# Row sums of a softmax gradient: from TensorE and PSUM to VectorE and SBUF, with a new instruction order for the whole program

## The chip, the core and the metric

The kernel runs on one core of one Trainium2 chip. Five engines of that core work side by side, each through its own list of instructions, in the order of that list: TensorE (PE, matmuls, which write PSUM), VectorE (DVE), ScalarE (ACT), GpSimd (POOL) and SyncE (SP, which here only starts transfers). The metric is the device time of one execution in microseconds (us), from the first to the last instruction and the little that lies around them. Lower is better.

## What is computed

The program is one transformer layer, forward, and the gradients of its inputs and weights. Sequence 2048, width 512, 32 heads of 16; each position attends to 8 positions, itself and those 2, 4, ... 14 before it.

```python
qkv = layernorm(x) @ wqkv                       # q, k, v per head
logits[h,s,w] = (q[h,s] . k[h,s-2w]) * scale    # w = 0..7, masked before the start
attn = softmax(logits, over w)
h  = x + (sum_w attn[h,s,w] * v[h,s-2w]) @ wo
h2 = h + gelu(layernorm(h) @ w1 + b1) @ w2 + b2
# outputs: h2 and the gradients of x, wqkv, wo, w1, b1, w2, b2 for a given grad_out
```

The change lies in the backward softmax. With `da[h,s,w] = (grad of the attention output at s) . v[s-2w]`, the gradient of the logits is

```
pp = attn * da
glf = pp - attn * sum_w(pp)         which equals  attn * (da - sum_w pp)
```

## The kernel before

The 2048 rows are four chunks of 512. Per chunk the program has three stages. The forward attention stage makes the layer norm, q, k, v (`p1_qkv`), the logits and softmax (`p1_attn`), the weighted sum of v (`p1_o`) and h (`p1_h`). The MLP stage runs the MLP forward and backward (`p2_h`, `p2_out`, `p2_dg`, `p2_bwd`); its end is `ln_bwd` (L604 to L617), which leaves the gradient of h in the tile `ghr`. The last stage is the attention backward: `p3_go` (L946) multiplies `ghr`, turned by a DMA transpose, by wo and leaves `got`; `p3_dots` makes the softmax gradient; `p3_bands` makes the gradients of q, v and k; `p3_gl1` (L1045) brings them back to x, and `ln_bwd` finishes the tile `gx`, which is stored. The weight gradients (`wg_group`, L1071) are long accumulating matmuls that need no VectorE; they are placed between everything else.

No 8-wide dot product is a matmul here. VectorE multiplies two wide tiles (128 x 4096, tiles `prf`, `prb`, `prbo`, `prbq`, `prbv`, `prbk`, L517 and L557), and TensorE adds groups of partitions up by a matmul with a constant 0/1 matrix (`S`, L525 and L566), 8 or 16 matmuls of 32 output rows for each such product. A wide product occupies VectorE and is followed by a short matmul group that waits for it.

In `p3_dots`, for one chunk, four products `prb` (L517) and their sums (L525) leave `da` in two PSUM banks, `L`. Then:

- L966, VectorE: `pp` = `L` * `attn`, 1024 elements on 128 partitions, fp32 from PSUM, bf16 to SBUF.
- L972, TensorE: minus the sum of `pp` over w, as eight accumulating 128-column matmuls with `nident`, the negative identity. ScalarE copies the sum to the SBUF tile `sr` (L283, tag `rowsum`).
- L985, TensorE: two 512-column matmuls with `ident` add `sr`, repeated over w, onto `L`.
- L988, VectorE: `glf` = `L` * `attn`, again from PSUM.
- L541, ScalarE: `halos` copies a few columns of `glf` between partitions.

`glf` is transposed in blocks into `cfq` and `cfk` (L535), the factors of the products `prbq` and `prbk`.

What sets the order is no scheduler at run time. The whole program is first listed as small operations (`op`), and two tables of numbers written out at the end of the file decide: `ORDER` gives the order in which the operations are issued, for all engines at once, and `HOMES` the SBUF address or PSUM bank of every tile. Each engine then runs its own operations in that order. A wait arises where an operation needs a result of another engine, or where its tile lies on the place of an older tile that is still being read.

Of the kernel before, what the change touches and what calls it, by code (L numbers as in the profile page):

```python
# [10 lines left out]
P = 128  # L11
# [3 lines left out]
ALU = mybir.AluOpType  # L15
# [3 lines left out]
W = 8  # L19
# [129 lines left out]
def kernel(  # L149
# [105 lines left out]
    MM = 0.2157  # L255
# [5 lines left out]
    def tt_us(n, f32=False):  # L261
        return 0.07 + (1.04e-3 if f32 else 0.52e-3) * n
# [689 lines left out]
    def p3_dots(c):  # L952
# [8 lines left out]
        L = ps_("La", 2)  # L961
# [21 lines left out]
        def sub():  # L983
            for wh in range(2):
                T.matmul(L()[:, wh * 512:(wh + 1) * 512], lhsT=(nident if RSB else ident)[:], rhs=sr().unsqueeze(1).to_broadcast([P, 4, P]), start=False, stop=True,  # L985
                         skip_group_check=True)
        op("PE", 2 * MM, sub, r=[sr, NID if RSB else IDENT], w=[L], tag="subsum")
        op("DVE", tt_us(1024, True), lambda: V.tensor_tensor(out=glf()[:, c, :, 0:P], in0=L3(), in1=ac(), op=ALU.mult),  # L988
           r=[L, (attn, c)], w=[(glf, c)], tag="glf")
# [290 lines left out]
RSB = False  # L1280
# [169 lines left out]
```

## Time and profile before

| what | value |
|---|---|
| runs of the kernel | 544.49, 546.46, 546.56 us; median 546.46 |
| the profiled execution: its own time | 545.53 us |
| the profiled execution: its span | 543.8 us (1.7 us lie around it) |
| mean granted TensorE clock | 0.996 |
| busy: PE, DVE, ACT, POOL | 97%, 86%, 62%, 3% |
| bytes moved by DMA | 136.63 MB, mean 251 GB/s |

All rows that are quoted below come from that one execution. "PE" is matmul time, "PEld" the loading of the stationary matrix, which overlaps it; "SPq" is a transfer being issued. A group row gives the line, the engine, the operation, what it writes and reads, how often (x), its busy time and the mean length of one in ns, then the engine's idle time just in front and what ended it. In a timeline row the first number is the start, the second the length, both in us.

### The profile page before, as it was taken

How to read it: one execution, taken by the hardware profiler on the slowest of the kernel's cores; microseconds unless marked ns; L12 is line 12 of the kernel's file. 1: busy time of each engine (PE TensorE's matmuls, PEld its weight loads, DVE VectorE, ACT ScalarE, POOL GpSimd, SP SyncE). 2: the span in 40 equal slices, each digit the busy share in tenths (PEclk: the TensorE clock that was granted, in tenths of full speed). 3: DMA queues.
4: the chain of work that ended last, by engine and by line, in shares of the span. 5: the costliest groups of instructions: out<-in, count | busy, mean ns of one | idle time of the engine just before them, and what ended most of it. 6: DMA issues, size and time to landing. Idle time of an engine off the chain costs nothing.

```text
span 543.8 us, 8104 instructions
## 1 busy us (share of the span) xinstructions
PE 526.0 (97%) x3017; PEld 235.3 (43%) x3063; DVE 467.7 (86%) x599; ACT 339.0 (62%) x591; POOL 17.4 (3%) x23
## 2 busy tenths in 40 slices
PE   8699999999999999999999999999999999999995
PEld 3344434444444444444444444445544444433442
DVE  5969999999999999998670339899989999999973
ACT  6938878999999967896522423224254455444664
POOL 0310000200000100000000000000000000000003
PEclk9989999999999999999999999999999999999999
DMA  7898899998998999999999999999999899999987
GB/s 216 204 285 250 249 271 296 246 272 253 226 256 252 304 238 221 219 271 204 230 170 204 191 203 212 208 293 257 230 331 303 298 309 233 318 309 287 289 223 220
DMA packets 230872, 136.63 MB, mean 251 GB/s; under 512 B 188400, under 2 KB 218800, under 8 KB 226736
## 3 DMA queue, kind: packets, MB, share of 16 engines
q1 hardware_dynamic: 230448, 135.06, 97.2%
q0 software_dynamic: 384, 1.05, 0.7%
q8 instruction: 24, 0.39, 0.3%
q14 instruction: 16, 0.13, 0.1%
HBM read 54.73 MB, written 37.84 MB: 170 GB/s over the span
## 4 chain that ended last, share of the span: by engine, by line
PE 86%; DVE 4%; DMA 4%; ACT 2%; issue 2%; SPq 1%; POOL 0%; POOLq 0%; DVEq 0%; ACTq 0%
PE ps L1071 27%; PE ps L908 9%; PE ps L922 9%; PE ps L880 9%; PE ps L826 8%; PE ps L1045 8%; PE ps L566 6%; PE ps L674 4%; PE ps L946 3%; DVE prf L517 2%; PE ps L525 2%; DMA w<-in_B_w_dram 2%; PE ps L790 1%; DMA ln1T<-ln 1%; PE ps L699 1%
## 5 line engine op out<-in xcount | busy, mean ns | idle before, releaser
L908 PE MATMUL ps<-goT,w2T 128*128 128x512 bf16 x224 | 52.5, 379 | 0.1
L922 PE MATMUL ps<-w1T,xb 128*128 128x512 bf16 x217 | 51.3, 379 | 0.4
L880 PE MATMUL ps<-w,gl 128*128 128x512 bf16 x218 | 50.8, 379 | 0.7 <-DMA w<-in_B_w_dram 0.3
L826 PE MATMUL ps<-ln2T,w 128*128 128x512 bf16 x224 | 50.3, 379 | 0.1
L1045 PE MATMUL ps<-wqkvT,gqkvT 128*128 128x512 bf16 x187 | 43.7, 380 | 0.6 <-ACT gvs L571 0.2
L283 ACT CAST wgs<-ps 128x512 bf16<-128x512 f32 (+1 forms) x30 | 15.8, 561 | 45.0 <-PE ps L1071 45.0
L828 ACT ACTIVATE xb<-ps,b1c 128x512 bf16<-128x512 f32 x56 | 35.1, 689 | 10.1 <-PE ps L826 9.9
L910 DVE SCALAR_TENSOR_TENSOR xb<-xb,ps 128x512 bf16<-128x512 bf16 x56 | 36.7, 682 | 5.4 <-PE ps L908 4.9
L1071 PE MATMUL ps<-gw1in,ln 128*128 128x512 bf16 (+1 forms) x186 | 38.8, 352 | 0.3
L1071 PE MATMUL ps<-gor,gw2in 128*128 128x512 bf16 x162 | 38.6, 379 | 0.4 <-issue 0.2
L557 DVE TENSOR_TENSOR prbq<-Rq,cfq 128x4096 bf16<-128x4096 bf16 x16 | 36.0, 2287 | 1.4 <-PE ps L566 1.1
L557 DVE TENSOR_TENSOR prbv<-Rv,cfv 128x4096 bf16<-128x4096 bf16 x16 | 35.9, 2286 | 0.4 <-DMA Rv<-go_d 0.3
L557 DVE TENSOR_TENSOR prbo<-Ro,cfo 128x4096 bf16<-128x4096 bf16 x16 | 36.0, 2285 | 0.1
L517 DVE TENSOR_TENSOR prf<-qt,kt 128x4096 bf16<-128x4096 bf16 x16 | 36.0, 2280 | 0.0
L517 DVE TENSOR_TENSOR prb<-got,vw 128x4096 bf16<-128x4096 bf16 x16 | 35.8, 2285 | 0.2
L557 DVE TENSOR_TENSOR prbk<-Rk,cfk 128x4096 bf16<-128x4096 bf16 x16 | 35.8, 2284 | 0.0
L1071 PEld LDWEIGHTS <-ln 128*128 128x128 bf16 x256 | 24.5, 98 | 23.9 <-issue 1.7
L880 PEld LDWEIGHTS <-gl 128*128 128x128 bf16 x224 | 21.7, 98 | 27.4 <-issue 1.5
L908 PEld LDWEIGHTS <-w2T 128*128 128x128 bf16 x224 | 21.9, 98 | 26.6 <-issue 0.4
L922 PEld LDWEIGHTS <-xb 128*128 128x128 bf16 x224 | 21.9, 98 | 26.5
L826 PEld LDWEIGHTS <-w 128*128 128x128 bf16 x224 | 21.5, 98 | 27.3 <-issue 2.4
L604 ACT ACTIVATE gyr<-ps,rstd 128x512 bf16<-128x512 f32 x28 | 19.0, 680 | 18.6 <-PE ps L1045 12.4
(164 smaller groups left out, 924.5 us busy)
## 6 DMA issues: line engine op xcount, KB each, us to landing
Ro<-v_d SPq DMA_DIRECT2D x4, 1280.0 KB, 7.3
Rq<-k_d SPq DMA_DIRECT2D x4, 1280.0 KB, 7.2
Rv<-go_d SPq DMA_DIRECT2D x4, 1280.0 KB, 6.3
Rk<-q_d SPq DMA_DIRECT2D x4, 1280.0 KB, 7.7
g_d<-gl SPq DMA_DIRECT2D x9, 512.0 KB, 4.0
gh_d<-xb SPq DMA_DIRECT2D x9, 512.0 KB, 4.2
Ro<-v_d SPq DMA_DIRECT2D x4, 1024.0 KB, 7.2
Rq<-k_d SPq DMA_DIRECT2D x4, 1024.0 KB, 8.5
```

The costliest lines, as they stand in the source:

```text
L517: op("DVE", tt_us(4096), lambda g=g, pr=pr: V.tensor_tensor(out=pr(), in0=ql()[:, g, :].unsqueeze(1).to_broadcast([P, W, 512]), in1=_sub(k ...
L557: V.tensor_tensor(out=pr().rearrange("p j a (d h) -> p (j a) d h", h=H), in0=_sub(R()[:, o0, 0:1], [[1024, 4], [st, 2], [1, 512]]), in1=_s ...
L566: T.matmul(ps()[32 * j:32 * j + 32, :], lhsT=S4[:], rhs=pr()[:, j, hf, :], start=(hf == 0), stop=(hf == 1), skip_group_check=True)
L674: T.matmul(ps()[:, gg * 512:(gg + 1) * 512], lhsT=_sub(wq_()[:, dc, 0:1], [[4, P]], g), rhs=cols_r(st_[c]["ln1T"], dc) if c in PM else col ...
L826: T.matmul(ps(), lhsT=w1()[:, dc, f * P:(f + 1) * P], rhs=cols(ln2T[c], dc, c in FM2), start=(dc == 0), stop=(dc == DC - 1))
L828: op("ACT", act_us(512, 1), lambda f=f, ps=ps, xb=xb, f0=f0: A.activation(out=xb()[:, f - f0, :], in_=ps(), func=ACT.Identity, bias=b1c[:, ...
L880: T.matmul(ps(), lhsT=d["g"][f // 4]()[:, f % 4, j * P:(j + 1) * P], rhs=w2()[:, f, :], start=(f == 0), stop=(f == FT - 1))
L908: T.matmul(ps(), lhsT=w2T()[:, dc, f * P:(f + 1) * P], rhs=cols(goT, dc, True), start=(dc == 0), stop=(dc == DC - 1))
L910: op("DVE", 0.61, lambda f=f, ps=ps, z=z, f0=f0: V.scalar_tensor_tensor(out=z()[:, f - f0, :], in0=z()[:, f - f0, :], scalar=1.0, in1=ps() ...
L922: T.matmul(ps(), lhsT=d["d"][f // 4]()[:, f % 4, j * P:(j + 1) * P], rhs=w1T()[:, f, :], start=(f == 0), stop=(f == FT - 1))
L1045: T.matmul(ps(), lhsT=gT()[:, j, b * P:(b + 1) * P], rhs=wqkvT()[:, k0 + b, :], start=(i == 0 and b == 0), stop=(i == 2 and b == 3))
L1071: T.matmul(ps()[:, 0:N], lhsT=l, rhs=r, start=(n == 0), stop=(n == k - 1))
```

## The change

The row sum and the subtraction move to VectorE and SBUF. `RSB = True` selects a branch that was there already: VectorE adds `pp` up over w with one `tensor_reduce` into `sr`. The two matmuls that added the sums onto `L`, and the product from PSUM, are replaced by two VectorE operations on bf16 tiles in SBUF: `glf` = `attn` * `sr`, then `glf` = `pp` - `glf`. The PSUM bank of the sums and ScalarE's copy are gone. Both tables are new from the first number to the last, so every engine's list changes, in all stages. In the changed file the lines behind L982 have numbers lower by three.

```diff
-        def sub():
-            for wh in range(2):
-                T.matmul(L()[:, wh * 512:(wh + 1) * 512], lhsT=(nident if RSB else ident)[:], rhs=sr().unsqueeze(1).to_broadcast([P, 4, P]), start=False, stop=True,
-                         skip_group_check=True)
-        op("PE", 2 * MM, sub, r=[sr, NID if RSB else IDENT], w=[L], tag="subsum")
-        op("DVE", tt_us(1024, True), lambda: V.tensor_tensor(out=glf()[:, c, :, 0:P], in0=L3(), in1=ac(), op=ALU.mult),
-           r=[L, (attn, c)], w=[(glf, c)], tag="glf")
+        gl = lambda: glf()[:, c, :, 0:P]
+        op("DVE", tt_us(1024), lambda: V.tensor_tensor(out=gl(), in0=ac(), in1=sr().unsqueeze(1).to_broadcast([P, W, P]), op=ALU.mult),
+           r=[sr, (attn, c)], w=[(glf, c)], tag="glfs", lock=1)
+        op("DVE", tt_us(1024), lambda: V.tensor_tensor(out=gl(), in0=pp(), in1=gl(), op=ALU.subtract), r=[pp], w=[(glf, c)], tag="glf", lock=1)
         halos(glf, c, "g")
...
-RSB = False
+RSB = True
...
 ORDER = (
-    7, 63, 64, 0, 10, 8, 65, 66, 4, 6, 42, 5, 26, 25, 3, 21, 24, 27, 22, 9, 30, 33, 28, 31,
...
 HOMES = (
-    608, 1115, 1883, 1024, 672, 2261, 2485, 1185, 701, 2261, 2117, 320, 1731, 288, 1121, 1603, 1796, 1989, 224, 160, 1925, 192, 128, 1024,
+    1365, 2673, 1925, 1024, 672, 2261, 2485, 1185, 701, 2261, 2117, 320, 1729, 288, 1121, 1603, 1796, 1989, 224, 160, 1601, 224, 128, 288,
```

Two places of VectorE's list show what the tables do around the change. The first is where the last stage begins. This is VectorE's list before; `u` and `ghr` belong to the MLP stage's `ln_bwd`, and `prb` are the first products of the attention backward (two chunks):

```order
L616 TENSOR_TENSOR u_1224_53_2915<-u_1224_53_2915,gor_39_1993 128x1024
L616 TENSOR_TENSOR u_1207_52_2879<-u_1207_52_2879,gor_39_1993 128x1024
L617 TENSOR_TENSOR ghr_1254_50_3002<-u_1128_46_2679,gyr_1020_46_2424 128x1024
L616 TENSOR_TENSOR u_1183_50_2823<-u_1183_50_2823,gor_38_1988 128x1024
L617 TENSOR_TENSOR ghr_1254_50_3002<-u_1183_50_2823,gyr_1061_49_2509 128x1024
L617 TENSOR_TENSOR ghr_1264_44_3021<-u_1224_53_2915,gyr_1150_48_2726 128x1024
L617 TENSOR_TENSOR ghr_1264_44_3021<-u_1207_52_2879,gyr_1151_48_2728 128x1024
L517 TENSOR_TENSOR prb_40_3051<-got_51_2783,vw_49_2473 128x4096
L517 TENSOR_TENSOR prb_41_3053<-got_51_2783,vw_49_2473 128x4096
```

And this is the same place of VectorE's list now:

```order
L617 TENSOR_TENSOR ghr_1240_51_2947<-u_1177_52_2804,gyr_1057_41_2500 128x1024
L517 TENSOR_TENSOR prb_50_2949<-got_53_2819,vw_43_2402 128x4096
L517 TENSOR_TENSOR prb_51_2951<-got_53_2819,vw_43_2402 128x4096
L617 TENSOR_TENSOR ghr_1240_51_2947<-u_1195_54_2843,gyr_1039_50_2472 128x1024
L1240 CAST gbb_46_3030<-gb_48_2788 128x18
L517 TENSOR_TENSOR prb_46_3032<-got_53_2819,vw_43_2402 128x4096
L517 TENSOR_TENSOR prb_47_3034<-got_53_2819,vw_43_2402 128x4096
L960 COPY vw_47_2784<-vw_48_2576 128x4x16
L616 TENSOR_TENSOR u_1237_51_2943<-u_1237_51_2943,gor_39_2164 128x1024
L616 TENSOR_TENSOR u_1230_51_2932<-u_1230_51_2932,gor_39_2164 128x1024
L617 TENSOR_TENSOR ghr_1287_43_3090<-u_1230_51_2932,gyr_1131_49_2685 128x1024
```

The first products have moved ahead of the last additions of the MLP stage, which now stand between and behind them; before, all eight `ghr` additions were through first. In TensorE's list 1,694 matmuls now stand ahead of the first sums of a `prb`, where 1,726 stood; the 32 that moved behind have 512 columns. At the other end, behind the last sums of a `prbk`, 96 matmuls of 512 columns now stand, where 84 stood. In all, TensorE's list has 3,023 matmuls instead of 3,063.

The second place is the softmax gradient of the first chunk on VectorE, before:

```order
L966 TENSOR_TENSOR pp_41_3126<-ps,attn_21_439 128x1024
L517 TENSOR_TENSOR prb_42_3134<-got_43_3059,vw_47_2488 128x4096
L517 TENSOR_TENSOR prb_42_3151<-got_43_3059,vw_47_2488 128x4096
L517 TENSOR_TENSOR prb_40_3171<-got_43_3059,vw_47_2488 128x4096
L988 TENSOR_TENSOR glf_39_3187<-ps,attn_21_439 128x8x128
```

And now:

```order
L966 TENSOR_TENSOR pp_40_3093<-ps,attn_26_470 128x1024
L976 TENSOR_REDUCE sr_40_3095<-pp_40_3093 128x128
L517 TENSOR_TENSOR prb_41_3097<-got_46_3044,vw_48_2576 128x4096
L517 TENSOR_TENSOR prb_45_3145<-got_46_3044,vw_48_2576 128x4096
L984 TENSOR_TENSOR glf_46_3147<-attn_26_470,sr_40_3095 128x8x128
L986 TENSOR_TENSOR glf_46_3147<-pp_40_3093,glf_46_3147 128x8x128
```

Between `pp` and `glf` stood three products that covered the way over TensorE and ScalarE; now two products stand there, the reduction behind `pp` and the two SBUF operations at the end, and nothing between `pp` and `glf` waits for another engine's result.

At the program's start ScalarE's first instruction is now the square root of L317, where it was a copy with an accumulated sum (L355); ahead of the first logits it loads two function tables instead of three. The load of `wq` is the 15th transfer in SyncE's list, where it was the 11th.

235 rows, old and new, of tables (HOMES, ORDER) are left out of this document.

## The prediction

> **What bounds the kernel now.** I read the page's first two parts, then the busy times by stretch, then the chain that ended last. The busy rows, and the same in 40 slices of the span:
>
> ```profile
> PE 526.0 (97%) x3017; PEld 235.3 (43%) x3063; DVE 467.7 (86%) x599; ACT 339.0 (62%) x591; POOL 17.4 (3%) x23
> ...
> PE   8699999999999999999999999999999999999995
> ...
> DVE  5969999999999999998670339899989999999973
> ```
>
> TensorE is busy in every slice but the first and last few, VectorE too, except around slices 18 to 23. So two engines are near their limit in the first and in the last third, and TensorE alone in the middle. Which of the two decides in the last stage, where the change lies, is seen in three stretches: before the first `prb`, from there to the end of the last `prbk`, and after it (columns: length; busy time of PE, PEld, DVE, ACT, POOL):
>
> ```profile
> 303.00:326.60 23.60, 23.50 (x109) 10.65 (x110) 4.94 (x9) 8.00 (x15) 0.00 (x0) 1.00 1.07 200
> 326.60:518.60 192.00, 189.62 (x1266) 84.03 (x1288) 184.08 (x126) 83.30 (x177) 0.00 (x0) 1.00 1.03 278
> 518.60:543.80 25.20, 19.01 (x102) 8.35 (x92) 13.22 (x27) 13.69 (x29) 4.35 (x8) 0.99 0.76 211
> ```
>
> In the 192.0 us of the last stage VectorE is idle for 7.9 us and TensorE for 2.4: they run in step, and neither has room for 5 us more unless the stage begins sooner. Just before it VectorE is idle for 18.7 of 23.6 us. The chain that ended last runs over TensorE:
>
> ```profile
> PE 86%; DVE 4%; DMA 4%; ACT 2%; issue 2%; SPq 1%; POOL 0%; POOLq 0%; DVEq 0%; ACTq 0%
> ```
>
> What VectorE waited for within the stage:
>
> ```profile
> DVE glf L988 <- PE ps L525: 2.3, 1, 2.3
> DVE glf L988 <- PE ps L985: 1.7, 1, 1.7
> DVE prbq L557 <- PE ps L566: 1.1, 1, 1.1
> DVE cfk L535 <- ACT glf L541: 1.0, 1, 1.0
> ```
>
> Half of its 7.9 us, 4.0, is `glf` waiting for TensorE. For the first chunk the round trip is seen in the timeline: `pp` at 338.3, the copied sums at 345.6, `glf` at 348.4.
>
> ```profile
> 338.27 1.22 DVE L966 TENSOR_TENSOR pp<-ps,attn 128x1024 bf16<-128x1024 f32 x1 [0.34 <-PE ps L525]
> ...
> 345.64 0.27 ACT L283 CAST sr<-ps 128x128 bf16<-128x128 f32 x1 [1.10 <-PE ps L972]
> ...
> 348.37 1.22 DVE L988 TENSOR_TENSOR glf<-ps,attn 128x1024 bf16<-128x1024 f32 x1 [2.27 <-PE ps L525]
> ```
>
> **What leaves TensorE.** The matmuls that go, and a run of the wide ones for their true spacing (the group rows' means contain the pipeline's length, so I take the step from start to start):
>
> ```profile
> 345.00 0.61 PE L972 MATMUL ps<-pp,nident 128*128 128x128 bf16 x8
> ...
> 347.17 0.60 PE L985 MATMUL ps<-sr,ident 128*128 128x512 bf16 x2
> ```
>
> ```profile
> 204.94 8.63 PE ps L826 x40
> ```
>
> A wide matmul takes 8.63 / 40 = 0.216 us. Of the eight narrow ones each lasts 0.219 in its group row, so a step is (0.61 - 0.219) / 7 = 0.056 us; the group row:
>
> ```profile
> L972 PE MATMUL ps<-pp,nident 128*128 128x128 bf16 x32 | 2.4, 219 | 0.0
> ```
>
> Per chunk 8 x 0.056 + 2 x 0.216 = 0.88 us, for four chunks 3.5 us. TensorE works without a gap there, so all of it lies on the path as long as nothing else makes TensorE wait. ScalarE's copies go too (4 x 0.27 us); ScalarE is busy for 83 of 192 us here, so I cost that at nothing.
>
> **What comes to VectorE.** These rows price the removed product, the reduction (nearest row: the softmax's maximum, same shape but fp32 from PSUM) and the two bf16 operations in SBUF (nearest row: the softmax's division, same shape and repeated operand):
>
> ```profile
> L988 DVE TENSOR_TENSOR glf<-ps,attn 128x1024 bf16<-128x1024 f32 x4 | 4.9, 1220 | 3.9 <-PE ps L525 2.3 <-PE ps L985 1.7
> ...
> L739 DVE TENSOR_REDUCE mx<-ps 128x128 bf16<-128x1024 f32 x4 | 4.8, 1202 | 0.0
> ...
> L759 DVE TENSOR_TENSOR attn<-e,r 128x1024 bf16<-128x1024 bf16 x4 | 2.8, 690 | 0.2
> ```
>
> The reduction of bf16 in SBUF is in no row. From L988 to L759 the move from fp32 in PSUM to bf16 in SBUF cuts a product from 1.22 to 0.69; if the reduction gained as much it would cost 0.69, if nothing, 1.20. I take 1.20, the row of the same operation. Per chunk 1.20 + 2 x 0.69 - 1.22 = 1.36 us, in all 5.4 us (3.4 by the lower bound). The Trainium skill speaks against the change here: "VectorE: DVE Perf Modes", section "Rules for kernel authors", says to expect a `tensor_reduce` to run at one element per cycle, whatever its type or memory, and to restructure around it on a hot path. By that rule the lower bound falls away and the 5.4 us stand.
>
> **What the tables move.** VectorE's work between the first `prb` and the last `prbk` otherwise stays: by count, three `ghr` additions and one `u` move in, three `sx` reductions and one transposition of `cfv` move out, about as long. So the stage holds 184.1 + 5.4 = 189.5 us of VectorE work. Of the 7.9 us idle the 4.0 of `glf` should go: the chain from `pp` to `glf` lies on VectorE alone, and what it must still wait for is that older transfers have left the places of its tiles. With the other 3.9 us the stage lasts 193.4 us; the bounds are 189.5 (no wait) and 197.4 (other waits take the place).
>
> It can begin sooner. In the trace VectorE waits for a `u` of ScalarE, then for a transfer or matmul to free a place, and begins the products at 326.65, while the first `got` was there at 304.6:
>
> ```profile
> 303.54 1.07 ACT L293 CAST got<-ps 128x512 bf16<-128x512 f32 x2 [2.44 <-PE ps L946]
> ...
> 313.03 0.59 ACT L283 CAST wgs<-ps 128x512 bf16<-128x512 f32 x1 [5.18 <-PE ps L1071]
> ```
>
> ```profile
> 316.95 1.29 DVE L616 TENSOR_TENSOR u<-u,gor 128x1024 bf16<-128x1024 bf16 x2 [13.48 <-ACT u L610]
> 323.39 0.69 DVE L617 TENSOR_TENSOR ghr<-u,gyr 128x1024 bf16<-128x1024 bf16 x1 [5.15 <-PE ps L1071]
> ...
> 326.65 11.28 DVE L517 TENSOR_TENSOR prb<-got,vw 128x4096 bf16<-128x4096 bf16 x5
> ```
>
> Now the products stand ahead of these additions, and 32 wide matmuls fewer lie ahead of their sums: 32 x 0.216 = 6.9 us. If VectorE keeps that pace, the stage begins at 326.65 - 6.9 = 319.75 and its last product ends at 319.75 + 193.4 = 513.15.
>
> **The end.** The last product ended at 518.49 and TensorE's last matmul at 537.72, 19.2 us later:
>
> ```profile
> 514.00 4.49 DVE L557 TENSOR_TENSOR prbk<-Rk,cfk 128x4096 bf16<-128x4096 bf16 x2
> ```
>
> ```profile
> 531.51 6.21 PE L1071 MATMUL ps<-gks,ln1b 128*128 128x512 bf16 x28
> ...
> 536.57 2.08 POOL L273 DMA_DIRECT2D out_dram<-gx  x4 [1.12 <-DVE gx L617]
> 537.75 0.58 ACT L283 CAST wgsq<-ps 128x512 bf16<-128x512 f32 x1 [1.14 <-PE ps L1071]
> ```
>
> Twelve more wide matmuls now stand behind the last sums, 12 x 0.216 = 2.6 us, so TensorE ends 21.8 us after the last product: at 534.95, 2.8 us earlier than before. By TensorE's own work it could not end before 537.72 - 3.5 = 534.2, so the two accounts agree within a microsecond and VectorE's is the later one; I take that. Of the 6.1 us from the last matmul to the span's end I change nothing: the last copy of a weight gradient and the last `gx` stores were issued within a microsecond of each other, so shortening one leaves the other.
>
> **The start.** ScalarE loads one function table less there. The load of `wq` goes four places back:
>
> ```profile
> 4.66 1.28 ACT L382 ACT_TABLE_LOAD   x1
> ...
> 27.20 3.15 PE L674 MATMUL ps<-ln1T,wk 128*128 128x512 bf16 x8 [3.91 <-DMA ln1T<-ln]
> ```
>
> ```profile
> wq<-in_A_wqkv_dram SPq DMA_DIRECT2D x1, 512.0 KB, 5.5
> ```
>
> The 1.28 us saved lie ahead of the first normalised rows, but TensorE then waits 3.91 us for a transfer whose input ScalarE makes between evictions that need `wq`'s products. I bound the start between 1.3 us gained and 1.3 us lost (a late `wq`) and take nothing. The middle, where TensorE alone is the limit, keeps its work; I take nothing there either.
>
> **Sum.** 545.53 - 2.8 = 542.7 us against the profiled execution. The median of the runs lies 0.9 us above that execution; I add half of it: **543.2 us**, 0.6% under the median. A measurement of this kernel can tell about 0.5%, 2.7 us, from no change: the bounds are 543.7 and 549.2.
>
> **Rivals.** *Slower: the last stage does not begin sooner, and VectorE's added work is paid in full.* The mechanism is ScalarE's single list: the `u` and `got` that VectorE needs stand behind copies of weight gradients that wait for long matmul groups (the 5.18 us at 313.03). If the first product stays at 326.65, the last one ends at 326.65 + 193.4 = 520.05, the last matmul at 541.85, the time is 545.53 + 4.1 = 549.7; with `glf`'s idle time merely replaced, 553.7. The gain is gone once the first product starts later than about 322.5, and a loss can be measured from about 326 on. For it: the stage has 2.4 us of TensorE slack only. Against it: 15 us lie between the first `got` and the time needed.
>
> *No change that can be measured: other waits grow into the place of `glf`'s.* The stage lasts 197.4 us from 319.75, the last matmul ends at 538.95, the time is 546.8. For it: the new homes and transfers bring new waits, and VectorE's list has no slack to absorb one. Another way to the same place: the removed matmuls were worth nothing, because the array was not the limit, and VectorE's account breaks even; that gives 545.5. Its row is the 43% busy of weight loading against 97% of matmuls. The Trainium skill, "Perfetto Trace Analysis", section "Identifying the Most-Contended Engine", calls matmul busy time a poor measure and judges TensorE by weight loading. By that rule the array has room. The trace disagrees: 40 wide matmuls follow each other at 0.216 us, though each lasts 0.379, and 2,119 of that width alone make 457 us. I give that way 2 in 100.
>
> *More gained*: no wait left on VectorE and a quicker start, TensorE's 3.5 us and up to 1.3: 540.7.
>
> That the change does not do what it says is excluded by the order: both kinds of matmul are gone, four reductions are there.
>
> **Chances.** The forecast (541.3 to 545) 0.53, of which 0.40 lies under 543.7; more gained 0.08; no change 0.19; slower 0.20. So faster 0.48, same 0.32, slower 0.20. The range reaches from 540.0 to 549.7, the slower rival's likeliest price; the forecast's own range is 541.3 to 545.
>
> **What would show it.** Right: the first `prb` starts near 320, the last `prbk` ends near 513, `glf` waits for no matmul, reductions take 1.2 us, and 3.5 us of matmuls are gone. Wrong: a first `prb` near 326 (the slower rival), a stage longer than 197 us (other waits), or TensorE gaps in the first 140 us of over a microsecond more (a start that I took as even).

## The result, and the profile after

| kernel | median us | lowest to highest | runs |
|---|---|---|---|
| before | 545.86 | 543.70 to 548.90 | 20 |
| after | 541.31 | 538.50 to 545.33 | 20 |

The ratio of the times is 0.9922, with a 95% interval of 0.9907 to 0.9937: 0.78% faster, forecast 0.6%. The median of 541.31 us lies at the lower end of the range that was forecast (541.3 to 545). The profiled execution of after took 541.34 us, its span 539.6, its mean granted clock 1.000.

The busy rows of the page of after, and its slices of VectorE:

```profile
PE 524.6 (97%) x3023; PEld 233.1 (43%) x3023; DVE 476.6 (88%) x607; ACT 335.6 (62%) x586; POOL 15.6 (3%) x23
...
DVE  6889999999989999899741658999999999999993
```

VectorE works 8.9 us more than before (476.6 against 467.7), and its hole in the middle is fuller at its end, since the last stage begins earlier. The same three stretches of after, cut at its own first `prb` and last `prbk` (length; PE, PEld, DVE, ACT, POOL; granted clock, DMA share, GB/s):

```profile
303.00:317.20 14.20, 14.20 (x67) 6.47 (x66) 4.43 (x10) 7.09 (x15) 0.00 (x0) 1.00 1.16 202
317.20:513.90 196.70, 194.65 (x1278) 84.83 (x1280) 191.83 (x130) 82.62 (x172) 0.00 (x0) 1.00 1.05 281
513.90:539.60 25.70, 21.73 (x116) 9.50 (x104) 15.94 (x34) 14.95 (x32) 4.35 (x8) 1.00 0.77 217
```

The stage is 4.7 us longer than before (196.7 against 192.0), but it starts 9.4 us earlier. VectorE is idle in it for 4.9 us, TensorE for 2.05. VectorE's row at its start, and its first softmax gradient:

```profile
316.58 0.69 DVE L617 TENSOR_TENSOR ghr<-u,gyr 128x1024 bf16<-128x1024 bf16 x1 [6.43 <-PE ps L1068]
317.19 4.49 DVE L517 TENSOR_TENSOR prb<-got,vw 128x4096 bf16<-128x4096 bf16 x2
...
331.45 1.23 DVE L966 TENSOR_TENSOR pp<-ps,attn 128x1024 bf16<-128x1024 f32 x1 [1.89 <-PE ps L525]
332.71 1.92 DVE L976 TENSOR_REDUCE sr<-pp 128x128 bf16<-128x1024 bf16 x1
```

The first `prb` starts at 317.19 instead of 326.65. Its sums on TensorE, first before, then after:

```profile
336.24 1.91 PE L525 MATMUL ps<-prb,S 128*32 128x512 bf16 x32
```

```profile
329.42 1.91 PE L525 MATMUL ps<-prb,S 128*32 128x512 bf16 x32
```

They start 6.8 us earlier, and `pp`, which needs them, too (331.45 against 338.27). So of the 9.4 us by which the products start earlier, 6.8 reach `pp`. In the rest VectorE makes the additions that now stand behind the products and waits 1.89 us for these sums.

The three new operations by group:

```profile
L976 DVE TENSOR_REDUCE sr<-pp 128x128 bf16<-128x1024 bf16 x4 | 7.6, 1895 | 0.0
L984 DVE TENSOR_TENSOR glf<-attn,sr 128x1024 bf16<-128x1024 bf16 x4 | 2.8, 688 | 0.1
L986 DVE TENSOR_TENSOR glf<-pp,glf 128x1024 bf16<-128x1024 bf16 x4 | 2.7, 681 | 0.1
```

The reduction takes 1.90 us, not 1.20; the two others are as forecast. What VectorE still waited for between 314 and 515 us, longest first, shows no `glf` behind a matmul any more:

```profile
DVE ghr L617 <- PE ps L1068: 6.4, 1, 6.4
DVE pp L966 <- PE ps L525: 1.9, 1, 1.9
DVE prbv L557 <- DMA Rv<-go_d: 1.3, 2, 0.7
```

And the end of after, where the last stores of `gx` are issued from 531.29 us on, and the last copy of a weight gradient starts at 535.66:

```profile
525.97 9.66 PE L1068 MATMUL ps<-gks,ln1b 128*128 128x512 bf16 x44
...
531.29 2.08 POOL L273 DMA_DIRECT2D out_dram<-gx  x4 [2.77 <-issue]
...
535.66 0.59 ACT L283 CAST wgsq<-ps 128x512 bf16<-128x512 f32 x1 [0.65 <-PE ps L1068]
```

The last matmul ends at 535.63 (before 537.72), and 3.97 us later the span is over (before 6.08).

### The profile page after: what moved, and what is told of

It is laid out like the page before. It is cut to its first block, busy times and chain, and to the rows that moved or that the text cites. A ratio compares the mean times of both kernels' runs of the same rounds, so it can differ in the third digit from the quotient of the medians.

```text
span 539.6 us, 8072 instructions
## 1 busy us (share of the span) xinstructions
PE 524.6 (97%) x3023; PEld 233.1 (43%) x3023; DVE 476.6 (88%) x607; ACT 335.6 (62%) x586; POOL 15.6 (3%) x23
## 3 DMA queue, kind: packets, MB, share of 16 engines
q0 software_dynamic: 384, 1.05, 0.7%
## 4 chain that ended last, share of the span: by engine, by line
PE 67%; DVE 14%; DMA 8%; ACT 4%; issue 3%; SPq 2%; POOL 1%; DVEq 0%; ACTq 0%
PE ps L1068 21%; PE ps L826 8%; PE ps L908 7%; PE ps L922 7%; PE ps L1042 7%; PE ps L880 6%; PE ps L566 3%; DMA Rk<-q_d 3%; DVE prf L517 3%; DVE prbk L557 3%; PE ps L946 3%; SPq L268 2%; PE ps L525 2%; DMA gqkvT<-gvs 2%; DMA v_d<-tmv 1%
## 5 line engine op out<-in xcount | busy, mean ns | idle before, releaser
L908 PE MATMUL ps<-goT,w2T 128*128 128x512 bf16 x224 | 54.1, 379 | 0.9 <-DVE h2s L882 0.8
L908 PEld LDWEIGHTS <-w2T 128*128 128x128 bf16 x224 | 21.8, 98 | 27.9 <-issue 1.9
```

Source lines behind the costliest of these rows:

```text
L908: T.matmul(ps(), lhsT=w2T()[:, dc, f * P:(f + 1) * P], rhs=cols(goT, dc, True), start=(dc == 0), stop=(dc == DC - 1))
```

## The experiments

All ratios are to runs of before on the same chip; after stands at 0.9922 by the same measure, and 0.001 is 0.55 us. The edits are shown shortened: three dots stand for code left out, and where an edit moves places in `ORDER`, the names of the operations stand for their numbers. The theory with which I began (A) says that the operations by themselves cost time and that the new order pays for them. Its rivals say that the operations are the gain (B), or that TensorE alone sets the end (C).

### The new operations in the old order

```diff
 ORDER of before, place by place
-pp ... rowsum (PE), rowsum (ACT) ... subsum (PE) ... glf
+pp, rsumv ...                                      glfs, glf
```

> The new operations (reduction, two SBUF operations, no row sums on TensorE) in the order and the homes of before: the reduction stands right behind pp, the two others at the old place of glf; two tiles got another home. Theory A (both engines are full in the last stage, and the new tables pay for the change): the four reductions cost 1.90 us each in the trace of after, so VectorE gets 4 x (1.90 + 2 x 0.69 - 1.22) = 8.3 us of work, saves at most the 4.0 us that glf waited, and the stage begins where it did; it grows by 4 to 5 us, the time is 548 to 551 us, slower than before. Rival B (the operations are what gains, the tables only follow): TensorE has 3.5 us less, 542 to 543 us, as fast as after.

Measured: 550.97 us, ratio 1.0105 (1.0084 to 1.0126). B falls. The stage, with the stretches around it:

```profile
303.00:326.40 23.40, 23.40 (x111) 10.58 (x109) 4.71 (x10) 8.01 (x15) 0.00 (x0) 1.00 1.04 194
326.40:524.90 198.50, 189.56 (x1246) 81.56 (x1248) 192.12 (x133) 82.49 (x173) 0.00 (x0) 0.99 1.00 270
```

It begins at 326.4, as before, and lasts 198.5 us, 6.5 longer than before and 1.8 longer than in after. VectorE's work rose from 184.1 to 192.1 us, and TensorE, with less to do, now stands idle for 8.9 of the 198.5 us. What TensorE waited for there names the products:

```profile
PE ps L566 <- DVE prbq L557: 4.0, 2, 3.7
PE ps L525 <- DVE prb L517: 3.0, 3, 1.6
```

So the operations alone lose 5 to 6 us, and the tables bring back some 10.

### The first products late again

In the new order, the four first `prb` go back behind the last additions of the MLP stage; on the other engines nothing moves.

```diff
 VectorE's list
-prb, prb, ghr, gbb, prb, prb, vw, u, u, ghr, ghr, pp
+ghr, gbb, vw, u, u, ghr, ghr, prb, prb, prb, prb, pp
```

> After, with the first four prb products behind the last additions of the MLP stage, as they stood before; every other engine keeps its list, one prb tile gets another home. Theory F (the earlier begin of the last stage is what the new order brings): VectorE has to wait for the u of ScalarE at 326.5 us before the first product, the stage begins near 328 us instead of 317, its sums and pp come 8 to 9 us later, and with 196 us of length the time is 546 to 550 us, the gain gone. Rival G (the begin is not what counts, since TensorE is full and the sums of the first products waited until 329.5 us anyway): under 2 us lost, 541.3 to 543.3 us.

Measured: 552.68 us, ratio 1.0148 (1.0122 to 1.0175), 11.4 us slower than after and so more than F foresaw. VectorE's list there:

```profile
317.84 0.69 DVE L616 TENSOR_TENSOR u<-u,gor 128x1024 bf16<-128x1024 bf16 x1
326.43 0.69 DVE L616 TENSOR_TENSOR u<-u,gor 128x1024 bf16<-128x1024 bf16 x1 [7.90 <-ACT u L610]
327.21 1.29 DVE L617 TENSOR_TENSOR ghr<-u,gyr 128x1024 bf16<-128x1024 bf16 x2
328.42 2.29 DVE L517 TENSOR_TENSOR prb<-got,vw 128x4096 bf16<-128x4096 bf16 x1
332.86 6.69 DVE L517 TENSOR_TENSOR prb<-got,vw 128x4096 bf16<-128x4096 bf16 x3 [2.15 <-DMA out_dram<-wgs]
342.40 1.22 DVE L966 TENSOR_TENSOR pp<-ps,attn 128x1024 bf16<-128x1024 f32 x1 [2.85 <-PE ps L525]
```

The `u` of ScalarE holds VectorE up for 7.9 us, the first product starts at 328.4, and `pp` is 10.95 us later than in after (342.40 against 331.45). The last `prbk` ends at 524.0, 10.1 later. Of this, 2.15 us are the new home of a `prb`, which waits for an older store: that part is the experiment's own. G falls: TensorE ran out of matmuls ahead of these sums.

```profile
335.20 1.05 PE L525 MATMUL ps<-prb,S 128*32 128x512 bf16 x8 [5.82 <-DVE prb L517]
339.60 2.75 PE L525 MATMUL ps<-prb,S 128*32 128x512 bf16 x24 [3.36 <-DVE prb L517]
```

Behind these gaps the granted clock was 0.50 between 334 and 342 us, where after has 1.00. The last 24 sums took 2.75 us, where 24 such sums took 1.48 with the new operations in the old order, and from the end of the fourth product to `pp` 2.85 us passed, where after needs 2.03 us from the start of its sums. That is another 0.8 us, which before, whose first sums came without such a gap, does not pay. So about 8 of the 10.95 us at `pp` are the price of the late start itself, the 8 to 9 that F named. In after the products have some 2.5 us to spare: the fourth ended at 326.87, and the sums started at 329.42, when TensorE came to them. By these rows a start still earlier would not have helped.

Most of what the tables bring, about 8 of some 10 us, is here. The slower rival's mechanism, ScalarE's `u` ahead of the products, is real; the new order goes around it.

### What TensorE's work is worth

Three runs change only matmuls: in before the row sums are nearly left out; in after 16 wide matmuls are added, or left out.

```diff
 e7, before
-for w in range(W): T.matmul(pr_()[:, 0:P], lhsT=nident[:], rhs=pp()[:, w, :], ...)
+T.matmul(pr_()[:, 0:P], lhsT=nident[:], rhs=pp()[:, 0, :], start=True, stop=True)
...
-for wh in range(2): T.matmul(L()[:, wh * 512:(wh + 1) * 512], ...)
+T.matmul(L()[:, 0:16], lhsT=ident[:], rhs=sr()[:, 0:16], start=False, stop=True, ...)
 e4, after (wg_group, tags q and o)
+if n == 0: T.matmul(ps()[:, 0:N], lhsT=l, rhs=r, start=True, stop=True)
 e12, after (the same groups)
+if n == 0: continue
```

> Before, in its own order, with the TensorE work of the row sums nearly left out: one 128-column matmul instead of eight, one of 16 columns instead of the two wide ones, so 3.2 us less TensorE work and a shorter way to glf; VectorE's work is as before. The gradient of the logits is not subtracted rightly in it. Theory D (the two engines are level in the last stage, VectorE has its 184 us to do): glf's waits of 4.0 us shrink, VectorE's list sets the rest, 1 to 2.5 us gained, 543.4 to 545 us. Rival C (TensorE sets the end): 3.2 us gained, 542.6 us.

> After, with 16 extra matmuls of 512 columns (16 x 0.216 = 3.5 us): the first matmul of each weight-gradient group of wqkv and wo is issued twice, all of them in the last stage or behind it. The work that the change took from TensorE is so given back. Rival C (TensorE sets the end): 3.5 us lost, 544.8 us, nearly the whole gain. Theory A (VectorE sets the pace in the last stage, TensorE behind it): the 10 or so that lie within the stage are partly hidden, those behind it are paid: 1 to 2.5 us lost, 542.3 to 543.8 us.

> After, with 16 matmuls of 512 columns less (3.5 us): the first of the 16 matmuls of each weight-gradient group of wqkv and wo is left out, so these gradients lack a part of their sum. It is the opposite of the dose in the last stage, which cost 1.3 us. Theory D (TensorE and VectorE are level in the last stage, so relief of one alone is worth little): what lies behind the last product is gained, about 1.5 us, the rest is hidden behind VectorE: 1 to 2 us gained, 539.3 to 540.3 us. Rival C (TensorE alone sets the end): 3.5 us gained, 537.8 us.

Measured: without the sums in before 544.15 us, ratio 0.9979 (0.9967 to 0.9992), so 1.2 us gained of 3.2. With the dose 542.60 us, 0.9954 (0.9937 to 0.9970), 1.3 to 1.8 us lost of 3.5. With the relief 541.47 us, 0.9930 (0.9910 to 0.9950): nothing gained of 3.5. By the traces nearly all of these 16 matmuls lie within the last stage: the time from the last product to the last matmul changes by under 0.5 us. C falls. Theory D, that both engines are level, had foreseen 1 to 2 us for the relief, so it missed too. The stage with the relief:

```profile
317.30:514.40 197.10, 190.84 (x1245) 83.25 (x1266) 191.64 (x130) 83.54 (x174) 0.00 (x0) 1.00 1.05 280
```

It lasts as long as in after with VectorE as busy (191.6 us), while TensorE's idle time grew from 2.05 to 6.3 us. TensorE waits for products now:

```profile
PE ps L566 <- DVE prbk L557: 1.8, 5, 0.7
PE ps L566 <- DVE prbq L557: 1.3, 2, 0.9
PE ps L566 <- DVE prbv L557: 1.1, 2, 0.6
```

In after, TensorE's work alone does not set the length of the last stage, though it is busy for 194.65 of 196.7 us.

### What VectorE's work is worth

The row sum by three additions; the row sums back on TensorE with the subtraction left in SBUF; and the three additions together with TensorE's relief.

```diff
 e2 (and e13)
-V.tensor_reduce(out=sr(), in_=pp().rearrange("p w n -> p n w"), axis=mybir.AxisListType.X, op=ALU.add)
+V.tensor_tensor(out=s4(), in0=pp()[:, 0:4, :], in1=pp()[:, 4:8, :], op=ALU.add)
+V.tensor_tensor(out=s4()[:, 0:2, :], in0=s4()[:, 0:2, :], in1=s4()[:, 2:4, :], op=ALU.add)
+V.tensor_tensor(out=s4()[:, 0, :], in0=s4()[:, 0, :], in1=s4()[:, 1, :], op=ALU.add)
 e5
-rsumv (DVE), glfs, glf = pp - glfs
+rowsum (PE), rowsum (ACT), glfs, glf = pp + glfs
```

> After, with the row sum made by three bf16 additions (512, 256, 128 elements a partition) instead of one reduction; same place, same order of all else, three of the four sr tiles in other homes. From the 0.69 us of 1024 elements I estimate 0.36 + 0.20 + 0.13 = 0.7 us against 1.90, 4 x 1.2 = 4.8 us less VectorE work. Theory A (VectorE's length of the last stage sets the end there): 2 to 4.8 us gained, 536.5 to 539.5 us. Rival C (TensorE sets the end all through, VectorE's 8.3 us were covered): under 0.7 us gained, 540.6 to 541.5 us.

> After, with the row sums back on TensorE (32 matmuls of 128 columns, 1.8 us, and four ScalarE copies), but the subtraction left on VectorE in SBUF; a few VectorE operations of the softmax gradient stand in another order so that nothing waits for the sums. VectorE loses 4 x 1.90 = 7.6 us, TensorE gains 1.8 us. Theory A (VectorE sets the pace in the last stage): 1 to 4 us gained, 537 to 540 us. Theory D, formed on the runs so far (4.0 us less VectorE work gained under 1 us, 3.5 us more TensorE work cost 1.3 to 1.8: the two engines are level in the stage, each covers most of a small change of the other): between 540 and 542 us. Rival C (TensorE sets the end all through): 1.8 us lost, 543 us.

> The same 16 matmuls left out, and the row sum made by the three additions, which took 0.92 us instead of 1.90 (4.0 us less VectorE work) and alone gained 0.3 us. Theory D: relief of both engines is worth more than the two alone together: 3 to 4.5 us gained, 536.8 to 538.3 us, at least 1 us more than the relief of TensorE alone and that of VectorE alone add up to. Rival C: as the relief of TensorE alone, 537.5 us, and that one is at 537.8.

The additions took 0.92 us a chunk:

```profile
L977 DVE TENSOR_TENSOR sr<-pp 128x512 bf16<-128x512 bf16 x4 | 1.6, 402 | 0.0
L978 DVE TENSOR_TENSOR sr<-sr 128x256 bf16<-128x256 bf16 x4 | 1.2, 292 | 0.1
L979 DVE TENSOR_TENSOR sr<-sr 128x128 bf16<-128x128 bf16 x4 | 0.9, 226 | 0.1
```

That is 4 x (1.90 - 0.92) = 3.9 us less on VectorE, and the time was 540.99 us, ratio 0.9915 (0.9892 to 0.9937): 0.3 us under after, which is within the intervals. With both reliefs it was 540.82 us, 0.9921 (0.9889 to 0.9952). Theory A's own forecast for the relief (2 to 4.8 us) falls, and theory D falls for good: relieving both engines at once brought nothing either.

Where the 3.9 us went is seen in part. In the profiled execution of the three additions, its fastest at 538.65 us, the stage shrank from 196.7 to 194.1 us (first `prb` 316.6, last `prbk` until 510.7), and VectorE had new waits for places of its product tiles:

```profile
DVE prb L517 <- PE ps L1071: 1.2, 1, 1.2
DVE prb L517 <- PE ps L525: 0.6, 1, 0.6
```

In this trace TensorE is busy for 193.70 of the 194.1 us: once VectorE had less to do, TensorE's own work left no room. With both reliefs neither engine was full in the profiled execution: the stage lasted 194.8 us, with TensorE busy for 190.1 and VectorE for 188.2. VectorE waited for the first sums (1.9 us), for places of product tiles (2.0 us) and for a gather of `Rk` (0.8 us). So what one engine no longer did turned into waits. The other five executions of the three additions took 540.3 to 541.9 us and have no trace. With both reliefs six executions spread from 537.97 to 543.07 us at a clock of 0.999 and more, wider than the 3 to 4.5 us looked for. That the remainder goes to transfers was not shown: the transfer engines' share is 1.05 in this stage and after waits 1.3 us for `Rv`, but in the trace of the three additions this wait is gone.

With the row sums on TensorE the time was 544.52 us, ratio 0.9984 (0.9967 to 1.0001), 3.2 us slower than after, with 7.6 us less VectorE work and 1.8 us more TensorE work, and slower than each theory had foreseen (537 to 543 us). VectorE's waits grew instead, 4.9 us of them ahead of `prbq` alone:

```profile
DVE prbq L557 <- PE ps L566: 3.2, 1, 3.2
DVE prb L517 <- PE ps L1068: 2.7, 2, 1.4
DVE pp L966 <- PE ps L525: 1.9, 1, 1.9
DVE prbq L557 <- PE ps L946: 1.7, 1, 1.7
```

Some VectorE operations stand in another order in this run, so it does not tell the sums' price from that of the order.

### The price of the reduction

```diff
+reduce(far axis), reduce(near axis)   bf16 to bf16, bf16 to fp32, fp32 to bf16, all in SBUF, 1024 to 128
```

> After, with two fills and six reductions of 1024 to 128 elements a partition on VectorE behind its last instruction, where it is idle; read for their own length, not for the time. bf16 in SBUF, added up over the far axis (as the row sums are) into bf16 and into fp32, bf16 over the near axis into both, fp32 in SBUF over both axes. If the 1.90 us come from the stride of a 2-byte element, the near axis and fp32 take 1.2 us or less and the far bf16 ones 1.9; if they come from the bf16 result, only those into fp32 are quick; if from SBUF, all take 1.9.

The six durations, as shortest, middle and longest of each pair (the middle is their mean):

```profile
L1255 DVE TENSOR_REDUCE mo<-mb x2: 1220/1494/1769, 532.5 to 534.3; 128x128 bf16<-128x1024 bf16 x2
L1255 DVE TENSOR_REDUCE mp<-mb x2: 1220/1540/1859, 535.5 to 537.4; 128x128 f32<-128x1024 bf16 x2
L1255 DVE TENSOR_REDUCE mo<-mf x2: 1220/1541/1862, 538.5 to 540.4; 128x128 bf16<-128x1024 f32 x2
```

The first of the first pair, over the far axis, is the long one:

```profile
L1255 DVE TENSOR_REDUCE mo<-mb 128x128 bf16<-128x1024 bf16 x1 | 1.8, 1769 | 0.0
```

Over the near axis each takes 1.22 us, over the far one 1.77 to 1.86, for bf16 and fp32 alike: none of the three answers that I had written down. The type is not the cause, the axis in SBUF is.

### The start

Two runs put warming matmuls into the gap of before's start, one adds work to after's first stage.

```diff
 e8: the second warm(4) of before moves from the start into the gap at 23.3 us
 e11: the same, and
-WARM2 = (4, 4)
+WARM2 = (16, 4)
 e6, after (p1_v of chunks 1 to 3, p1_proj of q in chunk 1): the first matmul of 16 groups twice
```

> Before, with one change at its start: four of the 21 dummy matmuls that warm TensorE up stand in the gap of 3.9 us at 23.3 us, as four of them do in after, instead of at the very start. In the trace of before the granted clock fell to 0.61 in the 4 us behind that gap, which costs about 1.5 us there; in after it stayed at 1.00. Theory S (the start's clock is a part of what the new tables brought, and it lasts to the end): the mean clock rises from 0.994 to 0.998 or more and the time falls by 1 to 2 us, to 543.8 to 545 us. Rival E (whatever is gained at the start is given back by 140 us): the clock may rise, the time stays within 0.5 us, 545.3 to 546.3 us.

> Before, with the gap of 3.9 us at its start filled: one group of four warming matmuls is moved there and made sixteen (16 x 0.216 = 3.5 us). The run with four matmuls there gained 0.7 us, and its executions with a mean clock of 0.997 and more took 542.8 to 543.3 us, those at 0.992 to 0.996 took 544.3 to 547. Theory S (the drop of the clock behind the gap is what costs, and it lasts to the end): the clock stays at 0.998 or more in nearly all executions, and the time falls by 2 us or more, to 542.5 to 543.5 us. Rival H (fast executions and a high mean clock only go together): the clock rises and the time falls by under 1 us.

> After, with the same 16 extra matmuls of 512 columns (3.5 us), now in the first attention stage between 30 and 73 us: the first matmul of twelve v groups and four q groups is issued twice. Theory E (the start's lead of 4 us over before is given back by 140 us because VectorE sets the pace there): under 1.5 us lost, 541.3 to 542.8 us. Rival C (TensorE sets the end all through, an early microsecond is worth as much as a late one): 3.5 us lost, 544.8 us.

Measured: 544.63 us, ratio 0.9989 (0.9973 to 1.0005), with four matmuls in the gap; 544.70 us, 0.9991 (0.9975 to 1.0007), with sixteen. With the gap filled the clock was 0.995 to 1.000 in all twelve executions (before 0.990 to 0.996), but no gain can be measured; the six at 0.998 and more have a median of 544.7 us. So theory S falls and H stands: the clock can explain at most a small part of the 4.5 us. Neither profiled execution is free of a fall. With four matmuls a gap of 3.4 us remained, and the clock was 0.57 from 28 to 32 us. With sixteen it was 1.00 there, but 0.66 from 75 to 80 us, behind gaps of 0.7 and 1.3 us. The dose of 3.5 us in after gave 541.78 us, 0.9948 (0.9924 to 0.9972): 0.5 us lost by the medians, 1.4 by the ratios, as theory E had it, and not C's 3.5. Six rows show how a lead at the start goes away; the number in brackets behind the second busy time counts the weight loads, one for each matmul. First before, then after:

```profile
0.00:40.00 40.00, 33.25 (x167) 14.91 (x170) 29.26 (x65) 26.59 (x46) 6.67 (x11) 0.96 0.86 233
40.00:140.00 100.00, 98.34 (x644) 43.55 (x649) 98.28 (x101) 89.30 (x149) 4.99 (x3) 1.00 0.94 261
140.00:303.00 163.00, 162.32 (x743) 73.82 (x755) 137.92 (x276) 118.15 (x177) 1.38 (x1) 1.00 1.01 232
```

```profile
0.00:40.00 40.00, 35.00 (x188) 16.54 (x189) 32.52 (x66) 28.67 (x50) 4.73 (x11) 1.00 0.88 241
40.00:140.00 100.00, 97.33 (x640) 42.87 (x639) 98.01 (x102) 86.49 (x147) 5.10 (x3) 1.00 0.91 256
140.00:303.00 163.00, 161.65 (x749) 72.90 (x748) 133.91 (x269) 115.82 (x173) 1.43 (x1) 1.00 1.02 231
```

After is 19 matmuls ahead at 40 us (about 4 us if all were wide), 9 ahead at 140 us and 2 ahead at 303. Between 40 and 140 us VectorE is busy for 98 of 100 us in both. The rows fit that TensorE can't keep a lead over the products that it needs; the early dose, mostly not paid, fits too.

## Why the prediction was right

The forecast for a profiled execution was 542.7 us, measured were 541.34. That is a sum of errors that nearly cancel, so the closeness of the number is in part luck:

| term | forecast | measured | error |
|---|---|---|---|
| first `prb` starts | 319.75 | 317.19 | -2.6 |
| length of the stage | 193.4 | 196.7 | +3.3 |
| last product to last matmul | 21.8 | 21.75 | 0.0 |
| last matmul to the end of the span | 6.1 | 4.0 | -2.1 |

- **The stage begins sooner: right, and by the right cause.** The late first products show that this term carries most of the gain. Its size, 32 wide matmuls or 6.9 us, came out at the sums: they start 6.8 us earlier, and so does `pp`. The products themselves start 9.4 us earlier, when a `ghr` ahead of them had waited 6.43 us for the place of its tile, which the order cannot tell; the 2.6 us beyond the forecast bought nothing, as the sums were not due yet. So -2.6 and most of +3.3 in the table are one error of bookkeeping: the last product ended at 513.9, forecast 513.15.
- **What leaves TensorE: the count was right, its worth was not.** "All of it lies on the path as long as nothing else makes TensorE wait" is the step that failed. In the old order 3.2 us were worth 1.2; with the new operations in it TensorE stood idle for 8.9 us, waiting for products. In the new order 3.5 us of other matmuls were worth nothing. The forecast survived because its sum took VectorE's account, not this one.
- **What comes to VectorE: mis-sized.** The reduction cost 1.90 us, the forecast took 1.20, so 8.3 us came instead of 5.4. The row that I called nearest, a maximum, read its far axis from PSUM, where it costs 1.20. The rule in the Trainium skill, "VectorE: DVE Perf Modes", section "Rules for kernel authors", was the right warning: the type brought no gain, and three additions did the same in half the time.
- **The stage's length** missed by 3.3 us: 2.3 more of work (191.8 against 189.5) and 1.0 more of waits (4.9 against 3.9). Its 196.7 us lie just under the 197 that the prediction named as a sign of being wrong. Counted from `pp` to the last product's end it grew by 2.2 us, from 180.2 to 182.4, where the forecast let it grow by 1.4.
- **`glf` waits for no matmul: right.** The 4.0 us are gone; 1.9 us of `pp` and 1.3 of `Rv` stand in the list of waits in their place.
- **Twelve matmuls more behind the last sums: right** to 0.05 us.
- **"Of the 6.1 us from the last matmul to the span's end I change nothing" failed.** By the traces two chains end the span: the `gx` stores, some 25 us behind the last product (before 543.8 - 518.49 = 25.3, with the new operations in the old order 549.9 - 524.9 = 25.0), and the last weight gradient, 4.0 us behind the last matmul. I had taken them as level. As the twelve matmuls moved behind the last product, the second chain became the later one by itself, and the 6.1 us became 4.0. This is read from the rows, no run was made for it.
- **The start and the middle taken as even: right at 303 us, by another way.** There was a gain of about 4 us at 40 us, and it was given back.
- **The rivals.** The slower one did not come, but its mechanism did when the order was undone (7.9 us behind ScalarE's `u`), and its price of 549.7 us was near what the new operations took in the old order (550.97). The rule by which TensorE had room (the Trainium skill, "Perfetto Trace Analysis", section "Identifying the Most-Contended Engine") would make the removed matmuls worth nothing. In the last stage of after that is what was measured for 16 other matmuls, with TensorE busy for 99% of it; but the rule's reason, room on the array, is not borne out, since 3.5 us more cost 1.3 to 1.8 us. It is no proof that VectorE sets the length either, since 3.9 us less of its work gained next to nothing. In the old order the matmuls were worth 1.2 us of 3.2.

**What stays open** is why 3.9 us less VectorE work, alone or with less TensorE work, gained under a microsecond. Executions of one kernel differ by 2 to 7 us here, and one trace for each kernel does not show what the others waited for. The three additions gave the lowest median of the kernels that compute everything, but not one that this measurement tells from after.

## What to carry to other kernels

Where two engines run in step, a microsecond taken from one is worth what the other lets through, and that has to be tried on both sides: here a late start cost 11 us, about 8 of them for the lateness itself, while relief of either engine brought next to nothing. When operations and order change together, run the new operations in the old order first; here that told a loss of 5 us from a gain of 10. Price a moved operation by a row with the same memory and the same axis, and write the end of a program as the later of its chains, not as one tail.

## What the hardware showed

- A `tensor_reduce` of 1024 to 128 elements on 128 partitions took 1.22 us over the near axis and 1.77 to 1.90 over the far one in SBUF, for bf16 and fp32 alike; from fp32 in PSUM, over the far axis, a maximum took 1.20. The Trainium skill, "SBUF — State Buffer", section "Door 1: The DMA port swizzle (why `[64,N]` ≈ `[32,N]`)", says that SBUF is read in lines of 16 bytes and that an access which crosses to a new line pays a penalty. The two axes agree with that, though no run tried other strides; that PSUM shows no such cost is in these rows alone.
- Three bf16 additions of 512, 256 and 128 elements took 0.40, 0.29 and 0.23 us, half of the reduction they replace.
- The granted clock fell to 0.61 in the four microseconds behind a TensorE gap of 3.9 us, and to 0.50 for eight microseconds around gaps of 5.8 and 3.4 us in the run with the late products. It stayed at 1.00 where the gap at the start was filled; the program's time did not follow.
